# The sinks' part of a banded attention: from fp32 products a head to stacked fp32r products a pair of heads, with eight sinks beside a key block

## The chip, the cores and the metric

The kernel runs on one core of a Trainium2 chip. The metric is the device time of one execution in microseconds. The engines are TensorE (PE in the profile; its weight loads are PEld), VectorE (DVE), ScalarE (ACT), GpSimd (POOL) and SyncE (SP), which here only starts transfers. They run their own instruction queues in order and wait for each other by semaphores.

## What is computed

An attention with a few sink positions and a window, then two mixing blocks on its output. Two batches, 8 heads, 768 positions, 64 channels a head; `n_sink` is 4 and `window` 128.

```python
def _attn_ref(q, k, v, n_sink, window):
    scores = np.matmul(q, k.transpose(0, 1, 3, 2)) / np.sqrt(D)
    is_sink = pos[None, :] < int(n_sink)
    in_window = (rel >= 0) & (rel < int(window))      # rel = row - column
    scores = np.where(is_sink | in_window, scores, -1e9)
    a = np.exp(scores - np.max(scores, axis=-1, keepdims=True))
    a = a / (np.sum(a, axis=-1, keepdims=True) + 1e-09)
    return np.matmul(a, v)

def _moe_ref(x, w_in, w_spatial, b_spatial, w_out):   # on the heads side by side
    h = np.maximum(x @ w_in, 0.0)
    u, v = h[..., :512], h[..., 512:]
    v_n = (v - mean(v)) / np.sqrt(var(v) + 1e-06)
    return (u * (einsum('ts,bsd->btd', w_spatial, v_n) + b_spatial[:, None])) @ w_out

def _moe2_ref(x, w_tok1, w_tok2, w_ch1, w_ch2):
    h = np.maximum(x.transpose(0, 2, 1) @ w_tok1, 0.0) @ w_tok2
    u = x + h.transpose(0, 2, 1)
    return u + np.maximum(u @ w_ch1, 0.0) @ w_ch2
```

## The kernel before

*Attention.* `banded` works on 12 blocks j of 128 queries, 6 a batch (i = j mod 6). A block goes in two halves of four heads, so there are 24 groups g = 2j + ph. One loop over n from -3 to 25 is a software pipeline with a lag for each step: iteration n computes the scores of group n+3 (`qk`, L177, on TensorE; `scores`, L202 and L207, on DVE, which also gives the row minimum), the exponentials of group n+2 (`expo`, L223, on ACT, with the row sums), the reciprocal sums and the normalisation of group n+1 (`sums`, L184; `norm`, L234 on POOL for two heads, L238 on ACT for the other two), the transposes of group n and their copies out of PSUM (`a_transpose`, L253; `a_out`, L261 on ACT and L264 on DVE), and the products with the values of group n-1 (`pv`, L287). Each engine's queue has the order in which these lines are written (the schedule is by hand).

*Sinks.* A block with a predecessor (i > 0, ten of the twelve) needs the first positions of the sequence as well. The keys come from the host with `SK` = 16 sink keys behind each 128-key block, so a group of scores reads a run of 272 columns (288 where the ring of key blocks wraps). `norm` multiplies the sinks' weights by the reciprocal sums on POOL into a tile `eS` of 8 heads x 16 sinks = 128 columns (L242). In the odd iteration of a block `sinks` transposes `eS` (L296) into a PSUM tile that it shares by name ("fl", two slots) with the dense work, and ACT copies it to `aS` (L298). In the even iteration that follows, `sinks_mm` adds, for each of 8 heads, the product of `vs` (the sinks' values, with zeros where row and column belong to different heads, 128 rows deep, 64 columns of the head) with the whole of `aS` into the PSUM tile of the block (L306): fp32, two records each. `x_out` then writes the block's output as an fp32r high part (L315, ACT) and a low part (L316, DVE).

*Precision.* fp32r products round their operands, so the dense parts split each operand into a rounded high part and the remainder and add three products, high x high, high x low and low x high (`mm3`, L57 to L59). The attention's products are plain fp32.

*Around it.* Each iteration from -1 to 6 also prepares one weight slice (`pump`): three DVE operations on 512 columns (L464, L468, L471), and for the slice before it an ACT copy (L482) and a POOL subtract (L483) behind them. Dense work on finished blocks (`fill`, tiles psv and psu, L57 to L59) is put on TensorE's queue at the end of each iteration up to a fixed cost, so its place in the order doesn't depend on time. `step` runs pieces of a layer norm. Loads go by SP's queue, `load_v` with the sinks' values behind block 1 of each batch. What follows the loop is the dense part, `mlp`.

## Time and profile before

| | |
|---|---|
| time, median of 3 runs | 499.09 us (498.95 to 500.24) |
| profiled execution, its own time | 499.52 us |
| span of it, first to last instruction | 497.7 us |
| mean granted TensorE clock | 0.978 |
| TensorE, DVE, ACT, POOL busy | 95%, 56%, 35%, 29% of the span |

The profile is of one execution. A row of the groups by line gives the line, engine, operation, result and operands by the program's names, shapes, count, then the busy time in us, the mean of one in ns, and the idle time of the engine ahead of it. Matmuls overlap: a matmul's duration holds its way through the array, so its price in a stream is the spacing, which the chain of waits shows. A table by stretch gives from and to in us, the length, then busy time and count for PE, PEld, DVE, ACT and POOL in that order. A stretch's clock is the mean granted TensorE clock as a share of 2.4 GHz. A POOL or DVE duration may hold a wait for the other.

### The profile page before, as it was taken

How to read it: one execution, taken by the hardware profiler on the slowest of the kernel's cores; microseconds unless marked ns; L12 is line 12 of the kernel's file. 1: busy time of each engine (PE TensorE's matmuls, PEld its weight loads, DVE VectorE, ACT ScalarE, POOL GpSimd, SP SyncE). 2: the span in 40 equal slices, each digit the busy share in tenths (PEclk: the TensorE clock that was granted, in tenths of full speed). 3: DMA queues.
4: the chain of work that ended last, by engine and by line, in shares of the span. 5: the costliest groups of instructions: out<-in, count | busy, mean ns of one | idle time of the engine just before them, and what ended most of it. 6: DMA issues, size and time to landing. Idle time of an engine off the chain costs nothing.

```text
span 497.7 us, 7141 instructions
## 1 busy us (share of the span) xinstructions
PE 473.5 (95%) x2672; PEld 395.4 (79%) x2672; DVE 280.5 (56%) x631; ACT 176.5 (35%) x471; POOL 145.3 (29%) x164
## 2 busy tenths in 40 slices
PE   8589799999999999999999899999999999999994
PEld 7357588788888999998888578888888888888883
DVE  6989864675553489946979798765222211311112
ACT  4556677686754322235542222222101110011000
POOL 1453742354344557652543133222100000000000
PEclk9859899999999999999999999999999999999998
DMA  8844131402005022313544244221020000200002
GB/s 265 264 149 139 65 97 38 153 23 86 2 2 211 1 84 65 96 32 105 170 127 131 83 126 128 84 86 42 2 84 0 1 0 1 85 1 0 0 1 91
DMA packets 19788, 38.82 MB, mean 78 GB/s; under 512 B 1825, under 2 KB 8225, under 8 KB 19745
## 3 DMA queue, kind: packets, MB, share of 16 engines
q1 hardware_dynamic: 19312, 38.02, 24.1%
q8 instruction: 23, 0.38, 0.3%
q10 hardware_dynamic: 432, 0.26, 0.2%
q14 instruction: 21, 0.16, 0.1%
HBM read 35.13 MB, written 3.15 MB: 77 GB/s over the span
## 4 chain that ended last, share of the span: by engine, by line
PE 82%; DVE 13%; ACT 1%; issue 1%; DMA 1%; POOL 0%; POOLq 0%; ACTq 0%
PE pso L59 7%; PE pso L57 7%; PE pso L58 7%; PE psc L57 6%; PE psc L59 6%; PE psc L58 6%; PE pv L287 4%; PE psg L59 3%; PE psg L58 3%; PE psg L57 3%; PE sc L177 3%; DVE wi L468 2%; PE psu L57 2%; PE ps L59 2%; PE ps L57 2%; PE ps L58 2%
## 5 line engine op out<-in xcount | busy, mean ns | idle before, releaser
L630 DVE SCALAR_TENSOR_TENSOR hh<-psc,hh 128x512 fp32r<-128x512 f32 x36 | 24.9, 692 | 127.9 <-ACT hh L629 127.8
L629 ACT ACTIVATE hh<-psc 128x512 fp32r<-128x512 f32 x36 | 21.5, 597 | 157.1 <-PE psc L59 157.1
L59 PE MATMUL pso<-c2H,hh 128*128 128x512 f32 x144 | 56.3, 391 | 1.2 <-DVE hh L630 1.2
L57 PE MATMUL pso<-c2H,hh 128*128 128x512 f32 x144 | 56.8, 394 | 0.0
L58 PE MATMUL pso<-c2L,hh 128*128 128x512 f32 x144 | 56.1, 390 | 0.0
L471 DVE SCALAR_TENSOR_TENSOR wi<-rawi,wi 128x512 int32<-128x512 int32 (+2 forms) x46 | 41.2, 895 | 1.6
L223 ACT ACTIVATE e<-s,nm 128x144 f32<-128x144 f32 (+1 forms) x96 | 38.1, 399 | 4.0 <-DVE nm L207 4.0
L468 DVE SCALAR_TENSOR_TENSOR wi<-rawi,wi 128x512 int32<-128x512 int32 (+2 forms) x46 | 36.4, 791 | 1.6
L464 DVE TENSOR_SCALAR wi<-rawi 128x512 int32<-128x512 int32 (+2 forms) x46 | 32.8, 712 | 0.7 <-POOL c1L L483 0.6
L59 PEld LDWEIGHTS pso<-c2H,hh 128*128 128x128 f32 x144 | 27.0, 188 | 7.3 <-DVE hh L630 1.6
L57 PE MATMUL psg<-wsTH,vnH 128*128 128x384 f32 x96 | 32.1, 334 | 0.0
L58 PE MATMUL psg<-wsTL,vnH 128*128 128x384 f32 x96 | 32.1, 334 | 0.0
L59 PE MATMUL psg<-wsTH,vnL 128*128 128x384 f32 x96 | 32.1, 334 | 0.0
L58 PEld LDWEIGHTS pso<-c2L,hh 128*128 128x128 f32 x144 | 27.1, 188 | 5.4
L57 PEld LDWEIGHTS pso<-c2H,hh 128*128 128x128 f32 x144 | 27.1, 188 | 5.4
L177 PE MATMUL sc<-kr,q 64*128 64x272 f32 (+2 forms) x192 | 29.5, 424 | 1.1 <-DVE nm L207 0.7
L59 PE MATMUL psc<-u2H,c 128*128 128x512 f32 x72 | 28.0, 389 | 0.0
L57 PE MATMUL psc<-u2H,c1H 128*128 128x512 f32 x72 | 28.0, 389 | 0.0
L58 PE MATMUL psc<-u2L,c1H 128*128 128x512 f32 x72 | 28.0, 389 | 0.0
L59 PE MATMUL psc<-u2H,c1L 128*128 128x512 f32 x72 | 28.0, 389 | 0.0
L57 PE MATMUL psc<-u2H,c 128*128 128x512 f32 x72 | 28.0, 389 | 0.0
L58 PE MATMUL psc<-u2L,c 128*128 128x512 f32 x72 | 28.0, 389 | 0.0
(139 smaller groups left out, 1108.7 us busy)
## 6 DMA issues: line engine op xcount, KB each, us to landing
rawi<-in_moe_w_ch SPq DMA_DIRECT2D x24, 512.0 KB, 3.6
rawi<-in_moe_w_in SPq DMA_DIRECT2D x8, 512.0 KB, 4.7
kr<-in_k SPq DMA_DIRECT2D x11, 288.0 KB, 4.2
v<-in_v SPq DMA_DIRECT2D x12, 256.0 KB, 3.8
out_x<-o SPq DMA_DIRECT2D x12, 256.0 KB, 2.3
q<-in_q SPq DMA_DIRECT2D x11, 256.0 KB, 4.9
raws<-in_w_spT SPq DMA_DIRECT2D x6, 384.0 KB, 3.9
rawi<-in_moe_w_out SPq DMA_DIRECT2D x4, 512.0 KB, 5.0
```

Of the source, the lines that this page charges most:

```text
L57: self.nc.tensor.matmul(ps, lh, rh, start=(first and i == 0), stop=False)
L58: self.nc.tensor.matmul(ps, lh, rl, start=False, stop=False)
L59: self.nc.tensor.matmul(ps, ll, rh, start=False, stop=(last and i == n - 1))
L177: nc.tensor.matmul(o, q[r, p, :], k, start=True, stop=True)
L223: nc.scalar.activation(out=self.e[j][:, 4 * ph + c, :u], in_=s[:, c, :u], func=AF.Exp, bias=nm[:, c : c + 1], scale=-1.0, accum_out=sm[:, ...
L287: nc.tensor.matmul(ps[h * D : (h + 1) * D, p, :], w[:, (2 * p + h) * D : (2 * p + h + 1) * D], self.aT[g][c][:, 2 * x + h, :], start=(p == ...
L464: V.tensor_scalar(out=wi, in0=hi, scalar1=3, scalar2=0x3FFFFFFF, op0=ALU.logical_shift_left, op1=ALU.bitwise_and,)
L468: V.scalar_tensor_tensor(out=wi, in0=hi, scalar=-0x40000000, in1=wi, op0=ALU.bitwise_and, op1=ALU.bitwise_or)
L471: V.scalar_tensor_tensor(out=wi, in0=lo, scalar=29, in1=wi, op0=ALU.logical_shift_right, op1=ALU.bitwise_or)
L629: nc.scalar.activation(out=h, in_=ps, func=AF.Relu)
L630: nc.vector.scalar_tensor_tensor(out=l, in0=ps, scalar=0.0, in1=f32(h), op0=ALU.max, op1=ALU.subtract)
```

## The change

`SK` is 8. The sinks' values and weights are both split into a rounded part and a remainder, and the three products that `mm3` would add one after the other stand under each other along the contraction: 3 parts x 4 heads x 8 sinks = `SR` = 96 rows. The host gives `vs` with the same values in all three parts. `split_vs` (iterations 1 and 13) rounds it on ACT and writes the remainder into rows 32 to 63 on DVE; `load_v` puts the raw values into a slot of the pump's tiles. `norm` now normalises 136 columns in place where there are sinks, and `sink_parts` (even iterations of blocks with sinks, behind `v_step`) copies the sinks' weights out as rounded (ACT), rounded again (POOL) and remainder (POOL), in the order that meets the rows of `vs`. `sinks` makes two transposes, one for four heads, and one ACT copy of both; `sinks_mm` makes four fp32r products, one a pair of heads, 128 columns of `vs` with 128 of `aS`.

```diff
--- before.py
+++ after.py
@@ -22,7 +22,8 @@
 DTOK = 256
 DCH = 1536
 NF = DCH // P
-SK = 16
+SK = 8
+SR = 3 * 4 * SK
 KW = P + SK
 RING = 4
 NEG = 8.0e9
@@ -143,8 +144,18 @@
         self.vb[j] = self.ap.tile([P, DM], F32, name="v", tag="v", bufs=4)
         nc.sync.dma_start(out=self.vb[j], in_=self.v[b, i * P : (i + 1) * P])
         if i == 1:
-            self.vsb[b] = self.ap.tile([P, DM], F32, name="vs", tag="vs", bufs=1)
-            nc.sync.dma_start(out=self.vsb[b], in_=self.vs[b])
+            raw = self.sp.tile([P, DM], F32, name="vsraw", tag="tmp", bufs=4)
+            nc.sync.dma_start(out=raw[0:SR], in_=self.vs[b])
+            self.vsraw = raw
+
+    def split_vs(self, b):
+
+        nc = self.nc
+        raw = self.vsraw
+        t = self.vsb[b] = self.ap.tile([P, DM], F32R, name="vs", tag="vs", bufs=1)
+        nc.scalar.activation(out=t[0:SR], in_=raw[0:SR], func=AF.Copy)
+        r = slice(4 * SK, 8 * SK)
+        nc.vector.tensor_tensor(out=t[r], in0=raw[r], in1=f32(t[r]), op=ALU.subtract)
 
     def slots(self, j):
 
@@ -230,19 +241,22 @@
         nc = self.nc
         j, ph = divmod(g, 2)
         r = self.rs[g]
-        e = self.e[j][:, 4 * ph : 4 * ph + 4]
+        w = KW if j % NB else P
+        e = self.e[j][:, 4 * ph : 4 * ph + 4, 0:w]
         nc.gpsimd.tensor_tensor(
-            out=e[:, 2:4, 0:P], in0=e[:, 2:4, 0:P], in1=r[:, 2:4].unsqueeze(2).to_broadcast([P, 2, P]), op=ALU.mult
+            out=e[:, 2:4], in0=e[:, 2:4], in1=r[:, 2:4].unsqueeze(2).to_broadcast([P, 2, w]), op=ALU.mult
         )
         for c in range(2):
-            nc.scalar.activation(out=e[:, c, 0:P], in_=e[:, c, 0:P], func=AF.Copy, scale=r[:, c : c + 1])
-        if j % NB:
-            if ph == 0:
-                self.eS[j] = self.ap.tile([P, H, SK], F32, name="eS", tag="eS", bufs=2)
-            nc.gpsimd.tensor_tensor(
-                out=self.eS[j][:, 4 * ph : 4 * ph + 4], in0=e[:, :, P:KW],
-                in1=r.unsqueeze(2).to_broadcast([P, 4, SK]), op=ALU.mult,
-            )
+            nc.scalar.activation(out=e[:, c], in_=e[:, c], func=AF.Copy, scale=r[:, c : c + 1])
+
+    def sink_parts(self, j):
+
+        nc = self.nc
+        t = self.eS[j] = self.ap.tile([P, 2, 3, 4, SK], F32R, name="eS", tag="eS", bufs=1)
+        e = self.e[j].rearrange("p (g h) k -> p g h k", g=2)[:, :, :, P:KW]
+        nc.scalar.activation(out=t[:, :, 0], in_=e, func=AF.Copy)
+        nc.gpsimd.tensor_copy(t[:, :, 1], f32(t[:, :, 0]))
+        nc.gpsimd.tensor_tensor(out=t[:, :, 2], in0=e, in1=f32(t[:, :, 0]), op=ALU.subtract)
 
     def a_transpose(self, g):
         nc = self.nc
@@ -292,21 +306,21 @@
     def sinks(self, j):
 
         nc = self.nc
-        ps = self.pp.tile([P, 512], F32, name="fl", tag="fl")
-        nc.tensor.transpose(ps[:, 0:P], self.eS[j].rearrange("p h s -> p (h s)"), self.ident)
-        self.aS[j] = self.ap.tile([P, P], F32, name="aS", tag="aS", bufs=2)
-        nc.scalar.activation(out=self.aS[j], in_=ps[:, 0:P], func=AF.Copy)
+        ps = self.pp.tile([P, 2, P], F32, name="fl", tag="fl")
+        for g in range(2):
+            nc.tensor.transpose(ps[0:SR, g], f32(self.eS[j][:, g].rearrange("p t h s -> p (t h s)")), self.ident)
+        self.aS[j] = self.ap.tile([P, 2, P], F32R, name="aS", tag="aS", bufs=2)
+        nc.scalar.activation(out=self.aS[j][0:SR], in_=ps[0:SR], func=AF.Copy)
 
     def sinks_mm(self, j):
 
         nc = self.nc
         vs = self.vsb[j // NB]
         for p in range(NC4):
-            for h in range(2):
-                nc.tensor.matmul(
-                    self.ps_x[j][h * D : (h + 1) * D, p, :], vs[:, (2 * p + h) * D : (2 * p + h + 1) * D],
-                    self.aS[j], start=False, stop=True, skip_group_check=True,
-                )
+            nc.tensor.matmul(
+                self.ps_x[j][:, p, :], vs[0:SR, p * P : (p + 1) * P], self.aS[j][0:SR, p // 2],
+                start=False, stop=True, skip_group_check=True,
+            )
 
     def x_out(self, j):
         nc = self.nc
@@ -360,6 +374,9 @@
                 self.expo(n + LE)
             if 0 <= n < NG and ph == 0 and j % NB:
                 self.v_step(j)
+                self.sink_parts(j)
+            if n in (1, 13):
+                self.split_vs(n // 12)
             self.step()
             if n in PUMPS:
                 self.pump()
@@ -901,13 +918,15 @@
     )
     sinks = np.broadcast_to(k[:, 0:1, :, :, 0:SK], (B, NB, P, NC4, SK))
     v = np.asarray(inputs["v"]).transpose(0, 2, 1, 3)
-    vs = np.zeros((B, H, SK, H, D), v.dtype)
-    for h in range(H):
-        vs[:, h, :, h] = v[:, 0:SK, h]
+
+    vs = np.zeros((B, 3, 4, SK, 2, 4, D), v.dtype)
+    for h in range(4):
+        for g in range(2):
+            vs[:, :, h, :, g, h] = v[:, None, 0:SK, 4 * g + h]
     give("q", q)
     give("k", np.concatenate([k, sinks], axis=4))
     give("v", v.reshape(B, S, DM))
-    give("vs", vs.reshape(B, P, DM))
+    give("vs", vs.reshape(B, 3 * 4 * SK, DM))
     give("limits", np.array([inputs["n_sink"], inputs["window"]]).astype(np.int64))
     give("w_spT", np.asarray(inputs["moe_w_spatial"]).T)
     for name in _INS:
```

## Rows read from the trace of the kernel before

**Rows 1.** The page's first part: busy us (share of the span) x instructions.

```profile
PE 473.5 (95%) x2672; PEld 395.4 (79%) x2672; DVE 280.5 (56%) x631; ACT 176.5 (35%) x471; POOL 145.3 (29%) x164
```

**Rows 2.** By stretch: length, busy us and count by engine, granted clock, DMA.

```profile
20.00:30.00 10.00, 5.42 (x34) 2.94 (x35) 9.69 (x29) 6.30 (x23) 5.56 (x6) 0.78 0.61 190
30.00:36.00 6.00, 6.00 (x27) 4.74 (x28) 5.46 (x17) 2.97 (x12) 2.81 (x4) 0.51 0.28 87
...
61.00:145.00 84.00, 83.39 (x736) 68.02 (x734) 49.68 (x197) 57.29 (x195) 34.91 (x57) 1.00 0.18 59
```

**Rows 3.** Chain of waits by line: 7.5 to 57.5, then 61 to 145 us.

```profile
by line: DVE s L207 14.6%; DVE wi L468 13.7%; DVE wi L471 12.1%; DVE sc L202 9.9%; PE pv L287 7.1%; DVE r L184 5.3%; DVE wi L464 4.9%; DVE aL L264 4.8%; DVE xTL L316 3.7%; issue 3.5%; PE sc L177 3.2%; PE psv L58 2.6%; PE psv L57 2.6%; PE ps
...
by line: PE pv L287 18.5%; PE sc L177 15.5%; PE psu L57 8.9%; PE pv L306 8.3%; PE tr L253 8.2%; PE psv L57 8.0%; PE psu L59 6.9%; PE psv L59 6.9%; PE psu L58 6.9%; PE psv L58 6.8%; ACT e L223 1.9%; PE fl L296 1.9%; ACT e L238 0.8%; issue 0.
```

**Rows 4.** Chain of waits in order (start us, us, what), 56 to 91 us.

```profile
57.46 0.41 PE fl L296
...
63.44 0.87 PE pv L306 x16
...
64.97 0.23 PE psv L59
...
65.56 0.17 PE psu L59
...
70.01 0.17 ACT aS L298
...
82.60 0.44 PE tr L253 x4
83.04 1.12 PE sc L177 x8
...
89.29 1.17 PE sc L177 x8
```

**Rows 5.** By stretch again, L306 alone, 57.5 to 145 us (PE, PEld, clock, DMA).

```profile
57.50:145.00 87.50, 8.35 (x128) 7.26 (x128) 0.99 0.18 57
```

**Rows 6.** Groups by line (busy us, mean ns of one, idle before), whole execution.

```profile
L58 PEld LDWEIGHTS psu<-xTL,wuH 128*128 128x128 f32 x64 | 12.0, 188 | 0.1
...
L306 PEld LDWEIGHTS pv<-aS,vs 128*64 128x64 f32 x160 | 9.1, 137 | 0.0
...
L298 ACT ACTIVATE aS<-fl 128x128 f32<-128x128 f32 x10 | 2.6, 257 | 0.7 <-PE fl L296 0.7
```

**Rows 7.** DVE in order of time (start us, us, what), 8 to 62 us.

```profile
20.88 0.42 DVE L464 TENSOR_SCALAR wi<-rawi 128x512 int32<-128x512 int32 x1
...
22.07 0.69 DVE L471 SCALAR_TENSOR_TENSOR wi<-rawi,wi 128x512 int32<-128x512 int32 x1
22.68 1.23 DVE L184 TENSOR_SCALAR r<-sums 128x4 f32<-128x4 f32 x1
...
27.63 1.63 DVE L471 SCALAR_TENSOR_TENSOR wi<-rawi,wi 128x512 int32<-128x512 int32 x1
```

**Rows 8.** ACT in order of time, the same stretch.

```profile
21.43 0.62 ACT L482 ACTIVATE wvH<-wi 128x512 fp32r<-128x512 f32 x1
```

**Rows 9.** POOL in order of time, the same stretch.

```profile
22.13 1.76 POOL L483 TENSOR_TENSOR wvL<-wi,wvH 128x512 fp32r<-128x512 f32 x1 [2.04 <-ACT wvH L482]
...
24.77 0.29 POOL L242 TENSOR_TENSOR eS<-e,r 128x64 f32<-128x64 f32 x1
...
27.10 1.62 POOL L483 TENSOR_TENSOR wvL<-wi,wvH 128x512 fp32r<-128x512 f32 x1 [0.81 <-ACT wvH L482]
```

**Rows 10.** The tile of the sinks' values, vs: its transfers and their landing.

```profile
L147 SPq DMA_DIRECT2D vs<-in_vs x2: 327/328/328, 10.8 to 86.1; - x2
...
DMA to landing us min/median/max: 2.6/4.9/7.2
```

**Rows 11.** Groups by line and shape of DVE alone, 8 to 60 us.

```profile
L207 DVE CUSTOM_DVE_ANT_0 s<-sc,m 128x144 f32<-128x144 f32 x36 | 9.7, 305 | 0.6
...
L207 DVE CUSTOM_DVE_ANT_0 s<-sc,m 128x128 f32<-128x128 f32 x5 | 1.2, 286 | 0.2 <-PE sc L177 0.2
```


## The prediction

> **What bounds the kernel now.** I read the busy times first: TensorE is busy for 95% of the span and its weight loads for 79%, no other engine above 56% [rows 1]. That is an average, so next came the table by stretch [rows 2]. It shows two regimes in the only part that the change touches, the attention (up to 145 us). From about 8 to 57 us VectorE (DVE) is the full engine, 9.69 of 10 us in the third ten, while TensorE has holes. From 61 to 145 us TensorE is busy for 83.39 of 84 us and DVE for 49.68. The chain of waits says the same [rows 3]: ahead of 57.5 us its largest pieces are DVE's score and weight lines, behind 61 us it is nearly all TensorE. So there are two prices: in the first stretch a DVE microsecond counts and a TensorE one mostly doesn't, in the second it is the reverse. Behind 145 us the order of work is fixed and TensorE stays full, so what is won or lost before is handed on.
>
> An exception lies in the first stretch. From 30 to 36 us TensorE is the full one, at a granted clock of 0.51, that is at 1.2 of its 2.4 GHz [rows 2]. What starts that piece is a DVE result (the low part of x, L316), so it moves with DVE.
>
> **The change on TensorE.** *The products of the sinks* (L306). A block with a predecessor issues 8 fp32 products of 64 columns of weights, 16 records, and they take 0.87 us on the chain [rows 4]. Of ten such blocks eight lie behind 57.5 us (x128 at 16 a block, [rows 5]); the other two lie where DVE decides. The new form is 4 fp32r products, 96 rows deep, 128 columns of weights, 128 moving columns. The trace has no fp32r product that narrow. Lower end: 384 moving columns go by in 0.17 us and 512 in 0.23 [rows 4], so 128 columns are 0.06 us of streaming. Upper end: no better than fp32, where two halves together take 0.87/4 = 0.22 us. Between them stands the weight load. An fp32r load of 128 columns is 188 ns against 137 ns for 64 columns in fp32 [rows 6]; if the difference is the 64 columns more, a column is 0.8 ns and 128 of them 0.10 us, longer than the streaming, so each product waits for its load. A transpose, load and one pass of 128 columns, goes by in 0.44/4 = 0.11 us too [rows 4]. I take 0.11: 4 x 0.11 = 0.44 a block, a gain of 8 x 0.43 = 3.4 us. The ends are 8 x (0.87 - 0.24) = 5.0 and nothing.
>
> The Trainium skill has a rule that would give the lower end ("TensorE: Matmul & The Clock Gate", section on weight-path perf modes): a fast weight load is on when there are 128 weights and the type is not fp32. If fp32r counts as "not fp32", the load would fall behind the streaming. The trace speaks against it, since the 128-column fp32r load is the longer one, 188 ns [rows 6].
>
> *The transpose of the sinks* (L296) becomes two, of 96 columns each. One more is 0.11 us by the same transposes; the bound above is half of the 0.41 us that the lone one takes at half clock [rows 4], 0.21. Seven lie behind 61 us: +0.8 us (up to 1.5). Two more, at 31.9 and at 57.46 us, lie on the chain at half clock (0.41 us for the lone one, [rows 4]): +0.2 each, +0.4 us. The one at 44 us lies beside DVE's work: nothing.
>
> *The scores* (L177) read 264 key columns for 272. Groups with 288 columns take 1.17 us, with 272 they take 1.12 [rows 4]: 16 columns are 0.05, so 8 are 0.025 us. 11 groups behind 61 us: -0.3 us.
>
> *The copy of the transposed sinks* (ACT, L298) reads 256 elements for 128. The old one is 257 ns [rows 6], so the new one is 0 to 0.26 us longer. It ends a wait of TensorE for its PSUM slot, at 70.01 us on the chain [rows 4]; elsewhere the slot comes back in time. I take the middle once, +0.1 us; if the copy came last in each of the seven late blocks it would be up to 1.8.
>
> Sum behind 61 us: -3.4 + 0.8 - 0.3 + 0.1 = -2.8 us.
>
> **The change in DVE's stretch.** *The split of the weights* (split_vs) is issued in iteration 1 and again in 13, behind the exponentials and ahead of the weight pump. DVE's subtract needs ACT's rounded copy. In iteration 1 DVE is through with its scores at 20.9 us and goes straight on with the pump [rows 7]. ACT ends its exponentials at 21.43 and goes on with the pump's 512-element copy, 0.62 us [rows 8]; a copy of the same width now comes first, to 22.05. So DVE stands still for 1.15 us and then subtracts for 0.7 us (the price of its 512-element operations, as L471 at 22.07 us, [rows 7]): the pump's operations start at 22.75, not at 20.88. Behind the waiting DVE queue the three weight operations, the reciprocal sums of the next group, its scores, and with these ACT's and GpSimd's (POOL's) normalisation. What comes late next is POOL's subtract of the pump. It now starts at 22.65, not 22.13, and runs 1.3 us alone. Rows show that DVE's next operation on SBUF waits out such a subtract: L184 at 22.68 us takes 1.23 us and ends as POOL ends (22.13 + 1.76) [rows 7, 9], and so does L471 at 27.63. That stall is in the old time too; it now falls on L464, from 22.75 to 24.0, and the pump ends at 25.8, where the old order, stall included, was through with the sums at 23.9. Delay 2.0 us; at least the 1.15 + 0.7 less the part of the old stall that goes, say 1.3, at most 2.4. Nothing later takes it up: each wait from there to 57 us is behind a DVE result of that queue. The raw weights are no cause of a wait: their transfer, issued at 10.8 us, lands in 7.2 us [rows 10]. In iteration 13 the same work lies beside TensorE's, where DVE has some 34 us of slack [rows 2]: nothing. SP's queue no longer holds the second transfer, at 86.1 us [rows 10], until the old weights are read; that gains nothing either, since TensorE is full there.
>
> *The split of the sinks' weights* (sink_parts) adds in iterations 2, 4 and 6 (blocks 1 to 3) an ACT copy and two POOL operations; the POOL product of L242, 0.29 us [rows 9], goes for each group. The ACT copy waits for POOL's normalisation, which is done (24.2 + 0.6) long before ACT's exponentials. It puts the pump's copy, and with it POOL's subtract, back by some 0.25 us, and the two POOL operations of about 0.29 each fall on DVE's pump. Where the subtract holds DVE (27.10 to 28.72, L471 ending 29.26, [rows 7, 9]) a later subtract means a later DVE. From 0 (they fall into gaps) to 0.6 (DVE waits out both); I take 0.3 each, nearest to the 0.25 us by which the subtract moves: +0.9 us (0 to 1.8).
>
> The Trainium skill ("SBUF — State Buffer", section "Who interferes with whom") says that a DVE operation with two inputs in SBUF and a GpSimd operation that reads SBUF shut each other out for a whole instruction. By it alone, each of the six POOL operations would cost DVE its whole length and this term would be 1.8 us. The stall of L471 agrees [rows 7, 9]; that all six would come first at their meeting with DVE no row shows.
>
> *Narrower scores on DVE* (L207): 305 ns at 144 columns, 286 at 128, 36 of them [rows 11]: 10 ns each at 136, -0.35 us. The wider normalisation (136 columns for 128) costs ACT and POOL some 10 to 40 ns an instruction and lies behind DVE. The smaller transfers of keys and sinks gain nothing where no engine waits for them.
>
> Sum ahead of 61 us, with the cold transposes: 2.0 + 0.9 - 0.35 + 0.4 = +2.95 us.
>
> **Sum.** -2.8 + 2.95 = +0.15 us on the profiled execution's 499.52 us, 499.7. That execution lies 0.43 us above the median of the runs (499.09), so against the median: 499.2 us. By the bounds of its own terms (delay 1.3 to 2.4, POOL 0 to 1.8, late transposes 0.8 to 1.5) this case reaches from 499.2 - 0.7 - 0.9 = 497.6 to 499.2 + 0.4 + 0.9 + 0.7 = 501.2. Within 0.3%, about what a measurement of this kernel can tell from no change, is 497.6 to 500.6.
>
> **The rivals.**
> *A: a narrow fp32r product costs what fp32 costs* (slower). Then the change doesn't do what it says: 4 x 0.22 replaces 0.87, the gain of 3.4 is gone, and the second transposes and DVE's delay stay: 499.2 + 3.4 = 502.6 us. For it: no fp32r product below 384 columns is in the trace. Against: from 512 to 384 columns the price falls in proportion. It decides from 0.154 us a product ((0.154 - 0.11) x 32 = 1.4).
> *B: DVE's delay isn't handed on* (faster). In the half-clock piece at 30 to 36 us [rows 2] TensorE sets the end. If it runs there at full clock in the new order, some 2 to 3 us come back, which pays for the 2.0 + 0.9: 496.3 us. For it: the granted clock is 0.78, 0.51 and 1.00 in the three stretches of [rows 2], so it does change level around this piece, and the piece can fall otherwise. Against: the change gives TensorE more idle time ahead of it, not less.
> *C: streaming sets the price,* 0.06 a product: another 8 x 0.2 = 1.6 us, 497.6 us. It has the 188 ns of a weight load against it [rows 6]. The Trainium skill's fast weight load (above) would do this.
>
> **How the numbers follow.** Forecast 0.45, A 0.27, B 0.18, C 0.10. Faster by over 0.3%: most of B (0.17), half of C (0.05), a little of the forecast (0.04), 0.26. Slower: A (0.25) and the upper end of the forecast (0.07), 0.32. Within: 0.42. The range reaches to A's and B's times and leaves out some 0.2 beyond them: 496.4 to 502.8; the forecast's own is 497.6 to 501.2.
>
> **What would show it.** In the changed trace: the four fp32r products of a block spaced 0.11 us (0.06 is C, 0.22 A); a DVE subtract of the sink weights near 22 us behind a hole of about 1.1 us; the pump's subtracts on POOL some 0.3 us later in iterations 2, 4, 6; TensorE's full stretch starting about 3 us later than 57 us and, from there to the last x_out, shorter by 2.8. A stretch ahead of it that isn't longer, or a shorter run at half clock, makes the forecast wrong on the fast side; a wait of TensorE for the copies of the sinks in most late blocks, on the slow side.

## The result and the profile after

The changed kernel takes 495.19 us (median of 4 runs, 494.53 to 495.90) beside 499.29 us of the kernel before, measured with it (498.95 to 500.24): a ratio of 0.9909, 95% interval 0.9885 to 0.9934, so 3.3 to 5.7 us faster. The forecast was 499.2 us, and its range began at 496.4: the change is faster than the range allowed. The profiled execution of after took 494.53 us, 4.99 us less than that of before (499.52 us); its span is 492.7 us, the mean granted clock 0.984.

The first part of the page, against [rows 1]: busy us, share and instructions. TensorE has 110 products fewer and 4.6 us less busy time, and is still the full engine.

```profile
PE 468.9 (95%) x2562; PEld 391.6 (79%) x2562; DVE 279.7 (57%) x633; ACT 178.8 (36%) x483; POOL 146.7 (30%) x164
```

The table by stretch of after, with the columns of [rows 2] (busy us and count of PE, PEld, DVE, ACT, POOL, then the granted clock):

```profile
30.00:36.00 6.00, 5.46 (x33) 4.49 (x35) 5.83 (x17) 3.14 (x13) 3.31 (x3) 0.70 0.50 170
36.00:57.00 21.00, 18.18 (x140) 13.15 (x141) 20.35 (x65) 15.01 (x52) 14.61 (x18) 0.93 0.40 128
57.00:61.00 4.00, 4.00 (x34) 2.92 (x33) 2.82 (x15) 3.57 (x14) 2.77 (x3) 0.94 0.01 4
61.00:145.00 84.00, 83.20 (x650) 68.82 (x651) 51.69 (x200) 60.15 (x202) 36.72 (x58) 1.00 0.19 59
```

and two stretches of before that the prediction did not read:

```profile
36.00:57.00 21.00, 16.94 (x159) 12.52 (x159) 19.26 (x56) 13.10 (x44) 11.70 (x15) 0.98 0.40 129
57.00:61.00 4.00, 4.00 (x19) 3.00 (x16) 2.95 (x14) 2.96 (x12) 2.54 (x4) 0.66 0.02 6
```

Between 36 and 57 us DVE gets through 65 instructions where it got through 56: that stretch is ahead of the old order, not behind it. And the two pieces in which TensorE ran at or near half clock, 0.51 at 30 to 36 us [rows 2] and 0.66 at 57 to 61 us, now have 0.70 and 0.94.

To see where the time goes I compare one event in every run: the start of the transposes of iteration n on TensorE (tile tr, in TensorE's order of time). In before it lies at 24.84 us for n = 3, 35.89 for n = 4, 60.69 for n = 8 and 138.72 for n = 23. The table gives each profiled execution's difference to that, in us, and the kernel's median beside the median of before measured with it. All the kernels of the next section stand in it.

| kernel | n = 3 | n = 4 | n = 8 | n = 23 | median | before | ratio (95%) |
|---|---|---|---|---|---|---|---|
| after | +1.60 | -0.60 | -2.49 | -5.03 | 495.19 | 499.29 | 0.9909 (0.9885 to 0.9934) |
| e1_split | +2.18 | +2.26 | +2.27 | +2.23 | 501.46 | 499.36 | 1.0040 (1.0021 to 1.0058) |
| e2_parts | +0.07 | -1.28 | -2.19 | -2.21 | 496.52 | 499.36 | 0.9935 (0.9911 to 0.9958) |
| e3_before_warm | +0.03 | -2.64 | -3.14 | -3.16 | 497.55 | 499.36 | 0.9950 (0.9931 to 0.9968) |
| e4_after_warm | +1.90 | +1.75 | +0.03 | -2.32 | 494.73 | 499.36 | 0.9901 (0.9873 to 0.9930) |
| e5_sub_later | -1.03 | -0.20 | -2.71 | -3.74 | 495.80 | 500.25 | 0.9917 (0.9902 to 0.9932) |
| e5_parts_late | +2.22 | +0.90 | +1.92 | -0.60 | 498.61 | 500.25 | 0.9951 (0.9930 to 0.9971) |
| e6_flush_late | -0.02 | -2.59 | -1.42 | -1.41 | 499.37 | 500.25 | 0.9996 (0.9981 to 1.0010) |
| e7_pe_only | -0.78 | -3.28 | -3.95 | -6.68 | 494.86 | 500.25 | 0.9908 (0.9889 to 0.9928) |
| f1_before_next | -1.78 | -4.40 | -3.06 | -3.08 | 497.66 | 499.37 | 0.9957 (0.9939 to 0.9976) |
| f2_after_next | -0.39 | -1.16 | -4.72 | -7.19 | 493.37 | 499.37 | 0.9883 (0.9858 to 0.9908) |
| f3_after_next_warm | -0.32 | -3.07 | -5.77 | -8.29 | 490.99 | 499.37 | 0.9827 (0.9802 to 0.9852) |
| g1_sk8 | +0.03 | -1.19 | -1.28 | -0.72 | 499.57 | 499.73 | 0.9992 (0.9978 to 1.0006) |

In the row of after, half of the gain is made by iteration 8 (-2.49), where the forecast had +2.95, and half behind it (-5.03 + 2.49 = -2.54). The late half is as forecast: -2.8, or -2.4 up to this event, which the last block's products (0.43) follow. The early half has the wrong sign. These profiles are of single executions, which scatter around the median: that of e4 took 497.75 us, 3.0 more than its kernel's median, that of e2 498.14 us, 1.6 more. They scatter behind iteration 23 too, by up to 1.4 us: e3's span is 1.8 us shorter than that of before (495.9 for 497.7) though its iteration 23 starts 3.16 us earlier, f3's 9.0 us shorter with 8.29.

**The late half.** The chain of waits in order, after (start us, us, what), at places that answer to [rows 4]:

```profile
54.53 0.59 PE fl L311 x2
...
60.91 0.59 PE pv L320 x4
61.51 0.28 PE psv L58
...
67.06 0.28 ACT aS L313
...
117.38 0.35 PE fl L311 x2
```

and in before what stood behind the products, and the lone transpose at full clock:

```profile
64.31 0.43 PE psv L57
...
100.36 0.26 PE fl L296
```

The products and the first dense product behind them took 0.87 + 0.43 = 1.30 us and take 0.59 + 0.28 = 0.87 us: 0.43 us less a block. Both have to be read, since the dense product takes longer on the chain behind the old products than behind the new ones. The second transpose costs 0.35 - 0.26 = 0.09 us. One stretch of TensorE's weight loads and two groups by line of after, against [rows 6]:

```profile
101.53 0.52 PEld L320 LDWEIGHTS pv<-aS,vs 96*128 96x128 f32 x4 [0.17 <-issue]
...
L320 PEld LDWEIGHTS pv<-aS,vs 96*128 96x128 f32 x40 | 5.2, 190 | 1.7 <-issue 0.9 <-ACT e L234 0.7 <-ACT e L250 0.2
L313 ACT ACTIVATE aS<-fl 96x256 fp32r<-96x256 f32 x10 | 3.6, 363 | 0.8 <-PE fl L311 0.8
```

Four loads of 190 ns go by in 0.52 us: they are (0.52 - 0.19)/3 = 0.11 us apart. The copy of the transposed sinks takes 363 ns, 0.11 more than the old one.

**The early half.** DVE in order of time, after, with the hole and the subtract that the change adds, the pump behind it, and then the low part of x (xTL) in iterations 2, 4 and 6 with what stands around it:

```profile
21.84 0.68 DVE L158 TENSOR_TENSOR vs<-vsraw,vs 32x512 fp32r<-32x512 f32 x1 [1.13 <-ACT vs L156]
22.55 1.42 DVE L481 TENSOR_SCALAR wi<-rawi 128x512 int32<-128x512 int32 x1
...
29.20 0.69 DVE L488 SCALAR_TENSOR_TENSOR wi<-rawi,wi 128x512 int32<-128x512 int32 x1
29.81 0.68 DVE L330 TENSOR_TENSOR xTL<-pv,xTH 128x512 fp32r<-128x512 f32 x1
30.41 0.65 DVE L195 TENSOR_SCALAR r<-sums 128x4 f32<-128x4 f32 x1
...
40.20 0.69 DVE L488 SCALAR_TENSOR_TENSOR wi<-rawi,wi 128x512 int32<-128x512 int32 x1
40.81 0.68 DVE L330 TENSOR_TENSOR xTL<-pv,xTH 128x512 fp32r<-128x512 f32 x1
...
52.56 0.68 DVE L330 TENSOR_TENSOR xTL<-pv,xTH 128x512 fp32r<-128x512 f32 x1
```

The same places in before, beside [rows 7]:

```profile
29.19 0.68 DVE L316 TENSOR_TENSOR xTL<-pv,xTH 128x512 fp32r<-128x512 f32 x1
...
37.16 0.69 DVE L264 TENSOR_TENSOR aL<-tr,lowT 128x512 f32<-128x512 f32 x1 [1.53 <-ACT aT L261]
...
40.06 1.68 DVE L468 SCALAR_TENSOR_TENSOR wi<-rawi,wi 128x512 int32<-128x512 int32 x1
...
42.38 0.68 DVE L316 TENSOR_TENSOR xTL<-pv,xTH 128x512 fp32r<-128x512 f32 x1
...
53.57 1.64 DVE L471 SCALAR_TENSOR_TENSOR wi<-rawi,wi 128x512 int32<-128x512 int32 x1
55.13 0.68 DVE L316 TENSOR_TENSOR xTL<-pv,xTH 128x512 fp32r<-128x512 f32 x1
```

POOL in order of time, after, beside [rows 9], and then the POOL operation that stands ahead of xTL in iteration 6 of before:

```profile
28.49 0.84 POOL L259 TENSOR_TENSOR eS<-e,eS 128x64 fp32r<-128x64 f32 x1
29.31 1.73 POOL L500 TENSOR_TENSOR wvL<-wi,wvH 128x512 fp32r<-128x512 f32 x1
...
40.31 1.74 POOL L500 TENSOR_TENSOR wuL<-wi,wuH 128x512 fp32r<-128x512 f32 x1
...
53.04 1.61 POOL L534 TENSOR_TENSOR vnL<-vf,vnH 128x512 fp32r<-128x512 f32 x1 [0.81 <-ACT vnH L533]
```

In before, the pump's POOL subtract of iteration 2 starts at 27.10 us, ahead of DVE's last pump operation (27.63), which then takes 1.63 us instead of 0.69 [rows 7, 9], and xTL stands behind it. Iterations 4 and 6 have such a stall too, each in its own form. In 4 the middle one of the three pump operations waits (40.06), and the last one stands between it and xTL. In 6 the last one waits (53.57), and what holds it is not the pump's subtract but the layer norm's, L534 at 53.04. These are three stalls of 0.94 to 0.99 us, each in DVE's queue ahead of an xTL, for which TensorE's next products with the values wait. In after the new POOL subtract of the sinks' weights (L259, itself drawn out to 0.84 us beside DVE's L485) stands first in POOL's queue. The pump's subtract starts at 29.31, behind the start of DVE's L488 at 29.20. That one now takes 0.69 us, xTL follows at once, and what waits out POOL is the reciprocal sum behind it (30.41, 0.65 us, ending with POOL at 31.04; in iteration 6 again, 1.08 us at 53.97), or, at 40.31, nothing. So xTL, 2 us late at the start, is 0.62 us late in iteration 2 and 1.57 and 2.57 us early in iterations 4 and 6. The Trainium skill ("SBUF — State Buffer", section "Who interferes with whom") says that the order of issue, not the kind of operation, decides which of the two blocks; these rows agree (0.69 us for the same DVE operation where it starts 0.11 us ahead of POOL's, 1.63 where it starts 0.53 us behind).

A stall behind xTL costs less, since DVE's queue has to wait there in any case: in before 1.53 us at 37.16, for ACT's copy of the next transposes, which TensorE reaches only at the end of the products that xTL starts (and 1.91 us at 61.96, behind the xTL of iteration 6).

In these two executions the early half adds up. Iteration 3 starts 1.60 us late, the price of the split. With the first stall moved, xTL is 0.62 late. TensorE then takes 4.74 us from its first products behind xTL to the transposes of iteration 4, where before took 5.97: 1.23 less, and iteration 4 starts 0.60 early. With the other two stalls gone, xTL is 1.57 and 2.57 early, and iteration 8 starts 2.49 early. So some 2.9 us come from the stalls and 1.2 from that piece of TensorE's.

### The profile page after: what moved, and what is told of

Same layout as the page of the kernel before. It is cut to its first block, busy times and chain, and to the rows that moved or that the text cites. A ratio compares the mean times of both kernels' runs of the same rounds, so it can differ in the third digit from the quotient of the medians.

```text
span 492.7 us, 6952 instructions
## 1 busy us (share of the span) xinstructions
PE 468.9 (95%) x2562; PEld 391.6 (79%) x2562; DVE 279.7 (57%) x633; ACT 178.8 (36%) x483; POOL 146.7 (30%) x164
## 4 chain that ended last, share of the span: by engine, by line
PE 77%; DVE 14%; ACT 5%; issue 2%; POOL 1%; POOLq 0%; ACTq 0%
PE pso L60 7%; PE pso L58 7%; PE pso L59 7%; PE psc L60 6%; PE psc L58 6%; PE psc L59 6%; PE psg L58 3%; PE psg L60 3%; PE psg L59 3%; PE pv L301 3%; DVE wi L485 2%; PE ps L60 2%; PE ps L59 2%; PE ps L58 2%; ACT e L234 2%; PE psu L58 2%
## 5 line engine op out<-in xcount | busy, mean ns | idle before, releaser
L488 DVE SCALAR_TENSOR_TENSOR wi<-rawi,wi 128x512 int32<-128x512 int32 (+2 forms) x46 | 40.3, 876 | 1.6
L234 ACT ACTIVATE e<-s,nm 128x136 f32<-128x136 f32 (+1 forms) x96 | 37.6, 393 | 3.9 <-DVE nm L218 3.9
L485 DVE SCALAR_TENSOR_TENSOR wi<-rawi,wi 128x512 int32<-128x512 int32 (+2 forms) x46 | 36.4, 790 | 1.6
L481 DVE TENSOR_SCALAR wi<-rawi 128x512 int32<-128x512 int32 (+2 forms) x46 | 32.5, 707 | 1.4 <-POOL c1L L500 1.2
L188 PE MATMUL sc<-kr,q 64*128 64x264 f32 (+2 forms) x192 | 28.7, 417 | 0.4 <-DVE nm L218 0.2
```

Of the source, the lines that this page charges most:

```text
L188: nc.tensor.matmul(o, q[r, p, :], k, start=True, stop=True)
L234: nc.scalar.activation(out=self.e[j][:, 4 * ph + c, :u], in_=s[:, c, :u], func=AF.Exp, bias=nm[:, c : c + 1], scale=-1.0, accum_out=sm[:, ...
L481: V.tensor_scalar(out=wi, in0=hi, scalar1=3, scalar2=0x3FFFFFFF, op0=ALU.logical_shift_left, op1=ALU.bitwise_and,)
L485: V.scalar_tensor_tensor(out=wi, in0=hi, scalar=-0x40000000, in1=wi, op0=ALU.bitwise_and, op1=ALU.bitwise_or)
L488: V.scalar_tensor_tensor(out=wi, in0=lo, scalar=29, in1=wi, op0=ALU.logical_shift_right, op1=ALU.bitwise_or)
```

## The experiments

The first theory after the result was that the delay of `split_vs` is real and handed on, and that something in the early stretch gives back more: either the two POOL operations, by where they put the pump's subtract, or the clock in the piece from 30 to 36 us. The first four kernels take these one at a time. Of each edit the text shows the lines that matter; `...` stands for the rest, and what stands behind a # is a note of this text.

**e1_split**: before, with the work of `split_vs` alone. The raw values land in a slot of the pump's tiles, and iterations 1 and 13 issue

```diff
...
+nc.scalar.activation(out=t, in_=raw, func=AF.Copy)
+nc.vector.tensor_tensor(out=raw[32:64], in0=raw[32:64], in1=t[32:64], op=ALU.subtract)
```

> The kernel before with the weights' split alone: the sinks' values are loaded into a pump tile, ACT copies them (512 columns) and DVE subtracts 32 rows x 512 columns in iterations 1 and 13, at the places of the change; the products stay fp32. Theory 'handed on' (the prediction's step): DVE's delay of 2.0 us in iteration 1 reaches the end, 501.3 us against 499.3. Rival 'taken up': the delay moves GpSimd's pump subtracts and TensorE's clock so that most of it comes back by 60 us, within 1 us of the kernel before.

Measured: 501.46 us, +2.1. The delay is there from iteration 3 on and stays to the end within 0.1 us (+2.18, +2.26, +2.27, +2.23): nothing takes it up. The term of the forecast (+2.0) holds, size and handing-on both (1.0 to 2.9 us by the interval).

**e2_parts**: before, with the ACT copy and the two POOL operations of `sink_parts` at their places, their results unused:

```diff
...
+nc.scalar.activation(out=t[:, :, 0], in_=e, func=AF.Copy)
+nc.gpsimd.tensor_copy(t[:, :, 1], f32(t[:, :, 0]))
+nc.gpsimd.tensor_tensor(out=t[:, :, 1], in0=e, in1=f32(t[:, :, 0]), op=ALU.subtract)
```

> The kernel before with the sinks' weights split beside (one ACT copy and two GpSimd operations of 128x64 in the even iterations of blocks with sinks, behind v_step, results unused; GpSimd's old product for the sinks stays too). Prediction's step: +0.9 us, 500.2. Rival 'the subtract is moved past DVE's operations': the pump's subtract of iterations 2, 4 and 6 starts later and meets DVE operations that it doesn't hold, so about 1 us a stall goes in two or three of them: -1 to -2 us, 497.3 to 498.3.

Measured: 496.52 us, 2.8 us less for added work. DVE in order of time, of this kernel, in iterations 2 and 4, then POOL in iteration 2:

```profile
27.70 0.69 DVE L481 SCALAR_TENSOR_TENSOR wi<-rawi,wi 128x512 int32<-128x512 int32 x1
28.32 0.68 DVE L325 TENSOR_TENSOR xTL<-pv,xTH 128x512 fp32r<-128x512 f32 x1
...
39.58 1.66 DVE L481 SCALAR_TENSOR_TENSOR wi<-rawi,wi 128x512 int32<-128x512 int32 x1
...
27.12 0.73 POOL L156 TENSOR_TENSOR eD<-e,eD 128x64 fp32r<-128x64 f32 x1
27.80 1.73 POOL L493 TENSOR_TENSOR wvL<-wi,wvH 128x512 fp32r<-128x512 f32 x1
```

Iteration 2 has the pattern of after without its delay: POOL's subtract at 27.80 for 27.10 [rows 9], DVE's operation at 27.70 with 0.69 us for 1.63 [rows 7], xTL at 28.32 for 29.19. Iteration 6 has it as well, with xTL at 52.95 for 55.13. In iteration 4 this execution still has its stall, 1.66 us at 39.58, and xTL's 41.16 for 42.38 is only what was won before. So two of the three stalls moved here, some 1.9 us; TensorE's piece behind the first xTL gave 0.4 more (5.56 us for 5.97); together they are the -2.19 of iteration 8. The kernel's executions lie between 495.23 and 499.13 us; that the faster ones have lost the stall of iteration 4 too is likely but not shown. The edit also leaves the tile eS one buffer for two, for which POOL waits 0.97 us at 31.51; after has one buffer as well, and so has e5_parts_late below, which loses the gain. These POOL operations are the step of the forecast that failed: their term was +0.9.

**e3_before_warm** and **e4_after_warm**: unused products with the identity ahead of `pv` in the early iterations, to see what the clock is worth, in before and in after.

```diff
...
+WARM = {0: 6, 1: 8, 2: 8, 3: 10, 7: 10}
...
+            if n in WARM:
+                self.warm(WARM[n])
```

> The kernel before with unused fp32 products of the identity (6, 8, 8, 10 and 10 of 128x128) ahead of the value products in iterations 0, 1, 2, 3 and 7, where TensorE has holes. Theory 'clock': the half-clock pieces at 30 to 36 and 57 to 61 us run at full clock, 12 products at 0.2 us and some more, -2 to -3 us, 496.3 to 497.3. Theory 'the clock decides little': within 0.7 us of the kernel before, or slower by what the fillers take.

> The changed kernel with the same fillers. If the clock explains some 2 us of what the change gained, this one gains less from the fillers than the kernel before does (-1 us, 494.2) and the two filled kernels differ by about 2 us only. If the clock explains nothing, both gain or lose alike and they differ by the 4.1 us of the change.

Measured: 497.55 us, 1.8 us less than before by the medians (1.6 to 3.4 by the ratio's interval), and 494.73 us (0.9901), no more than after gains without the fillers (0.9909). The stretch from 30 to 36 us of e3, then the fillers of iteration 3 in e4, in TensorE's order of time:

```profile
30.00:36.00 6.00, 6.00 (x58) 4.79 (x60) 5.80 (x18) 3.81 (x14) 2.74 (x4) 1.00 0.30 90
...
29.72 4.62 PE L338 MATMUL warm<-ident 128*128 128x128 f32 x20
```

In e3 the fillers hold the clock at 1.00 here and at 57 to 61 us, so the 1.8 us are the worth of both half-clock pieces in before, less than what the forecast's rival B had for the first alone (2 to 3). Iteration 4 starts 2.64 us earlier, but its xTL only 1.62 (40.76 for 42.38). In e4's profiled execution the fillers themselves ran at half clock (0.51 from 29.72 to 34.27 us), took 4.62 us where e3's took 2.50, and held up the products behind xTL until 34.27 us. The two kernels with fillers differ by 2.8 us, the two without by 4.1. That lies between what was expected if the clock explains 2 us of the gain and if it explains nothing.

**e5_sub_later** and **e5_parts_late**: after, with one of the two early edits moved. In the first, DVE's subtract of the split comes an iteration later, so that it doesn't wait for ACT; in the second, the two POOL operations of `sink_parts` are issued behind the pump.

```diff
# e5_sub_later
...
-        nc.vector.tensor_tensor(out=t[r], in0=raw[r], in1=f32(t[r]), op=ALU.subtract)
...
+            if n in (2, 14):
+                self.split_low()                 # the same subtract
# e5_parts_late
...
+            if 0 <= n < NG and ph == 0 and j % NB:
+                self.sink_parts_pool()           # behind pump(), no longer ahead of it
```

> The changed kernel with DVE's subtract of the split issued one iteration later (2 and 14, ACT's copy stays in 1 and 13), so DVE doesn't stand still for ACT. If a delay of DVE in iteration 1 reaches the end, as the split alone showed (+2.1 us), the hole of 1.1 us is saved: 494.1 us. If the rest of the change takes it up: no difference from 495.2.

> The changed kernel with the two GpSimd operations of sink_parts issued behind the pump instead of ahead of it; ACT's copy stays where it was. Theory 'the pump's subtract is moved past the operations that TensorE waits for': it starts earlier again, DVE stands still ahead of the low part of x in iterations 2 and 6, and most of what the parts alone gained (2.8 us) is lost: 497 to 498 us. Rival 'the gain of the parts comes from elsewhere' (the single eS tile, ACT's copy, chance in the clock): within 0.7 us of 495.2.

Measured: 495.80 us (0.9917, after 0.9909) and 498.61 us (0.9951, that is 2.1 us slower than after; the two intervals just meet). DVE in order of time, of e5_sub_later and then of e5_parts_late:

```profile
27.44 1.65 DVE L494 SCALAR_TENSOR_TENSOR wi<-rawi,wi 128x512 int32<-128x512 int32 x1
29.01 0.68 DVE L334 TENSOR_TENSOR xTL<-pv,xTH 128x512 fp32r<-128x512 f32 x1
...
29.82 1.63 DVE L496 SCALAR_TENSOR_TENSOR wi<-rawi,wi 128x512 int32<-128x512 int32 x1
31.37 0.68 DVE L336 TENSOR_TENSOR xTL<-pv,xTH 128x512 fp32r<-128x512 f32 x1
```

The second is the clean one: same work, same engine, only POOL's order, and the stall is back ahead of xTL in iterations 2, 4 (41.65, 1.65 us) and 6 (54.33, 1.63 us), with xTL at 31.37, 43.22 and 55.89 us where after has 29.81, 40.81 and 52.56. Of the first difference (1.56 us) 0.62 was there in iteration 3's start, ahead of the edit; the other 0.94 is the stall. TensorE's piece behind that xTL ran as in after (4.69 us at a clock of 0.69, for 4.74 at 0.68), so the clock does not make the difference. The order on POOL is the cause. The first was expected to win and did not: the hole is gone (iteration 3 is 2.63 us earlier than in after), but with it the chance of the meeting changed, the stall is back at 27.44 and again at 40.57 (1.65 us), the subtract now takes its 0.72 us in iteration 2 (25.50), TensorE's piece behind xTL took 5.95 us at a clock of 0.53, and by iteration 4 it is 0.40 us later than after. By iteration 8 it is 0.22 us ahead again, and then it loses 1.5 us up to iteration 23, nearly all of it in two waits of TensorE. One is for ACT's copy of the transposed sinks, for whose PSUM slot the dense products wait; TensorE in order of time, of this kernel:

```profile
68.03 0.44 PE L58 MATMUL psu<-xTH,wuH 128*128 128x384 f32 x1 [1.28 <-ACT aS L317]
```

After waits 0.57 us there. The other is for xTL at 107.28 us, 0.75 us for 0.16. An earlier start does not spare TensorE what ACT and DVE deliver late.

**e6_flush_late**: before, with the pump's ACT copy and POOL subtract issued behind `x_out`, to move the stall without adding work.

```diff
...
-            self.flush()
+            if hold:
+                self.held = self.half            # flushed behind x_out
...
```

> The kernel before with the pump's ACT copy and GpSimd subtract issued behind x_out instead of ahead of it, nothing added. Theory as above: the subtract can't stand between DVE and the low part of x, so the gain of the parts comes without them, 496 to 497.5 us against 499.3. Rival: within 0.7 us of the kernel before.

Measured: 499.37 us, no change. The edit did not do what it was made for, as DVE of this kernel shows:

```profile
27.61 1.75 DVE L476 SCALAR_TENSOR_TENSOR wi<-rawi,wi 128x512 int32<-128x512 int32 x1
```

The stall is still ahead of xTL (29.29), so it says nothing on that. It shows one other thing: its clock at 30 to 36 us was 1.00, for which nothing in the edit was meant, and iteration 4 started 2.59 us earlier, but its xTL only 1.46 (40.92 for 42.38). That is about the 1.53 us for which DVE had waited in before, and DVE has no more to give. By iteration 8 it is 1.42, and the time shows nothing of it. A gain by the clock in that piece is partly given back while DVE is the full engine.

**e7_pe_only**: after without the remainders: no subtract on DVE, no operation on POOL; the other two parts of the weights are zero.

```diff
...
-        nc.vector.tensor_tensor(out=t[r], in0=raw[r], in1=f32(t[r]), op=ALU.subtract)
...
-        t = self.eS[j] = self.ap.tile([P, 2, 3, 4, SK], F32R, name="eS", tag="eS", bufs=1)
-        nc.gpsimd.tensor_copy(t[:, :, 1], f32(t[:, :, 0]))
-        nc.gpsimd.tensor_tensor(out=t[:, :, 2], in0=e, in1=f32(t[:, :, 0]), op=ALU.subtract)
+        t = self.eS[j] = self.eS0                # set to zero once
```

> The changed kernel without the remainders: DVE's subtract of the weights and the two GpSimd operations of sink_parts are left out, the second and third part of the sinks' weights are zero, so the low-order terms are missing from the output; TensorE's work is that of the change. By the terms of the sum (late -2.8, narrower scores -0.35, cold transposes +0.4) it is 2.75 us faster than the kernel before: 496.6. By the two parts as measured alone (split +2.1, parts -2.8 of the change's -4.1) it is 3.4 us faster: 495.9, a little less for ACT's copies that stay.

Measured: 494.86 us (0.9908). From iteration 8 to 23 it gains 6.68 - 3.95 = 2.73 us: the late half again, and with the other kernels that have the new products (after 2.54, e4 2.35, e5_parts_late 2.52, f2 2.47, f3 2.52) the best-settled number of the study; only e5_sub_later, with its two waits, has less (1.03). Its early part gains 3.95 us, and not by the stalls, which all three stand ahead of xTL again (1.63 us at 26.96, 1.64 at 38.37 and 51.07). It ran at full clock there, 1.00 at 30 to 36 and at 57 to 61 us.

**f1_before_next, f2_after_next, f3_after_next_warm**: if the place of the stall is the cause, it can be moved on purpose. In before (f1) and in after (f2), the pump's POOL subtract of iterations 0 to 2 and 4 to 6 is issued one iteration later, behind the normalisation; f3 is f2 with the fillers of e4.

```diff
...
+            self.flush_low()                     # the POOL subtract held back, behind norm(n + LN)
...
-                self.pump()
+                self.pump(hold=n in (0, 1, 2, 4, 5, 6))
```

> The kernel before with the pump's GpSimd subtract (only that, in iterations 0 to 2 and 4 to 6) issued one iteration later, behind the normalisation of the next group, where DVE reads its scores out of PSUM; nothing added, ACT's copy stays. Theory 'what pays is where GpSimd's subtract meets DVE': the stalls of about 1 us on DVE go in six of seven iterations, the low part of x comes 2 us and more earlier, -2 to -4 us, 495.5 to 497.5. Rival 'it is the clock alone': no more than 1 us from the kernel before.

> The changed kernel with the same edit. By the theory most of the stalls that it had left (iterations 0, 3 and 5, and the one of 1.42 us on the first pump operation of iteration 1) go too: -1.5 to -3 us, 492.5 to 494; in the even iterations the value difference of GpSimd still meets the pump. If the change had already taken what there was to take: within 0.7 us of 495.2.

> The changed kernel with the same edit and the unused products that keep TensorE's clock up. If clock and stalls add, this is the fastest of all, 491.5 to 493; if DVE alone sets the end ahead of 60 us once the stalls are gone, it equals the one without the fillers.

Measured: 497.66, 493.37 and 490.99 us. DVE of f1, in order of time:

```profile
24.66 1.44 DVE L465 TENSOR_SCALAR wi<-rawi 128x512 int32<-128x512 int32 x1
...
27.47 0.68 DVE L316 TENSOR_TENSOR xTL<-pv,xTH 128x512 fp32r<-128x512 f32 x1
...
47.27 1.44 DVE L465 TENSOR_SCALAR wi<-rawi 128x512 int32<-128x512 int32 x1
48.74 1.64 DVE L469 SCALAR_TENSOR_TENSOR wi<-rawi,wi 128x512 int32<-128x512 int32 x1
```

With none of the change's work, before gains 2.1 us by its ratio: of DVE's six stalls beside POOL between 20 and 57 us four are left, and xTL of iteration 2 starts at 27.47 us for 29.19. The pump's last operation is free ahead of every xTL. But three of the four still lie in DVE's queue ahead of one, further forward (24.66 in iteration 2, 47.27 and 48.74 in iteration 6): at 24.66 and 47.27 POOL's product of the values (dv) meets the pump. So this run shows that fewer stalls pay, and not by itself that their place does. On after, the same edit gains another 1.3 us by the ratios (0.9909 to 0.9883), which their intervals do not tell from nothing. With the fillers as well the clock holds, 1.00 from 20 to 145 us, as f3 by stretch shows for one piece,

```profile
30.00:36.00 6.00, 6.00 (x54) 4.64 (x50) 5.83 (x18) 4.25 (x16) 4.16 (x5) 1.00 0.26 85
```

and that is worth 493.37 - 490.99 = 2.4 us. f3 is the fastest of all, 1.7% below before.

**g1_sk8**: before with eight sinks for 16 and nothing else; its fp32 products are 64 rows deep for 128.

```diff
-SK = 16
+SK = 8
+HS = 8 * SK
...
-                    self.aS[j], start=False, stop=True, skip_group_check=True,
+                    self.aS[j][0:HS], start=False, stop=True, skip_group_check=True,
```

> The kernel before with eight sinks beside a key block and nothing else: the fp32 products are 64 rows deep, 16 records a block as before, one transpose. By the prediction's rows: narrower scores on DVE -0.35 us, narrower key runs on TensorE -0.3 us, 498.7 against 499.3. If a product's price followed its depth, some 4 us more would go (495).

Measured: 499.57 us beside 499.73 (0.9992, interval 0.9978 to 1.0006). The narrower scores are worth less than the comparison can tell; the 0.35 + 0.3 us of the forecast lie within its interval. Halving the depth of the products is not worth anything that shows. In its profile iteration 4 starts 1.19 us earlier than in before with xTL at the same time, 29.19 us; that is the clock again (next section).

## Why the prediction was right and where it failed

**The products on TensorE: right.** The spacing is 0.11 us, the value taken; 0.06 (rival C) and 0.22 (rival A) are both refuted. A block saves 0.43 us, as forecast, with some luck: the four products take 0.59 us on the chain, not 0.44, and the 0.15 come back in the dense product behind them (0.28 for 0.43), which the sum left out. The argument from the weight load fits (at 190 ns a load is as long as those of [rows 6], and no faster); no run tests it apart from the spacing. The rule of the Trainium skill that would have given C ("TensorE: Matmul & The Clock Gate", section on weight-path perf modes) does not show here: if fp32r counts as "not fp32", 190 ns for 128 columns in fp32r against 137 for 64 in fp32 [rows 6] is no fast load, and the products stand 0.11 us apart, not at the 0.06 of streaming.

**The second transposes and the copy: right, in small.** 0.09 us against 0.11; the cold pair at 54.53 us in after takes 0.59 us for 0.41 [rows 4], +0.18 against +0.2. The copy is 0.11 us longer and stands on the chain of waits twice, at 67.06 and 77.25 us (once in before, [rows 4]); +0.1 was the term, taken once. The sum behind iteration 8 is -2.54 us where -2.4 was forecast for the same stretch.

**The split of the values: right.** The hole is 1.13 us (forecast 1.15), the subtract 0.68 (0.7), and the stall falls on L481 (1.42 us at 22.55), as written. Its price, alone, is +2.1 us and it is handed on to the end (e1_split).

**The POOL operations of the sinks: wrong in sign.** The term was +0.9 us and measured -2.8 (e2_parts; 2.1 to 4.4 less by the interval). The step that failed is the sentence "a later subtract means a later DVE". It priced the stall as if the subtract, moved back, would hold the same DVE operation until later. But a meeting of the two has an order: whichever starts first runs through. Moved back by 0.7 us in e2_parts and 2.2 in after (27.10 to 27.80 and 29.31), the subtract came behind the start of DVE's last pump operation, and the stall of 0.94 to 0.99 us went to the reciprocal sum behind xTL or nowhere, in all three iterations of after and in two of e2_parts. The row that could have told this was in view: DVE's L471 at 27.63 began only 0.53 us behind POOL's 27.10 [rows 7, 9], so the forecast's own shift of 0.25 us, together with the two POOL operations that it named "of about 0.29 each" and put ahead of the subtract, carried it past that start. The lower bound of the term should have been three stalls given back, -2.9 us, not 0. The rule on who shuts out whom, cited in the prediction, was used for the price (1.8 us) and not for the order.

**"Nothing later takes it up": true of the delay, wrong of the sum.** e1's delay is never taken up. In after it is, because the moved stalls give back more than the delay. The reason given, that each wait up to 57 us is behind a DVE result, passes over the wait of 1.53 us at 37.16, which is for ACT and TensorE: what comes late ahead of xTL is handed on, what comes late behind it need not be.

**Rival B** gave 496.3 us, the nearest, and the range, which was meant to reach to B's time, began 0.1 us above it. Its condition, the clock in the piece at 30 to 36 us, was half met (0.70 for 0.51). TensorE in order of time, before, then after, and behind these the stretch from the first products behind xTL of iteration 2 to the transposes of iteration 4 in before, after, e6_flush_late and g1_sk8:

```profile
29.92 0.69 PE L287 MATMUL pv<-aT,v 128*64 128x128 f32 x4 [1.97 <-DVE xTL L316]
...
30.55 0.69 PE L301 MATMUL pv<-aT,v 128*64 128x128 f32 x4 [1.05 <-DVE xTL L330]
...
29.92:35.89 5.97, 5.97 (x26) 4.71 (x27) 5.50 (x18) 2.97 (x12) 2.70 (x4) 0.51 0.28 88
...
30.55:35.29 4.74, 4.74 (x27) 3.95 (x28) 4.57 (x16) 3.07 (x12) 2.17 (x3) 0.68 0.51 170
...
30.02:33.30 3.28, 3.28 (x26) 2.67 (x27) 3.14 (x15) 2.95 (x12) 0.92 (x3) 1.00 0.49 160
...
29.93:34.70 4.77, 4.77 (x27) 3.71 (x27) 4.60 (x16) 2.94 (x12) 2.40 (x3) 0.64 0.38 110
```

TensorE is busy all through, with the same products but for one or two, and the time goes by the granted clock: 5.97 us at 0.51, 4.77 at 0.64, 4.74 at 0.68, 3.28 at 1.00. So the 1.2 us that after gains in this piece, in this execution, are the clock's. Whether the change raises that clock is not shown: e6 and g1 had 1.00 and 0.64 there with no edit that was meant for it. On the whole time it can have done little. The 71 executions of before under 502 us that stand beside the experiments took 498.2 to 498.7 us at a mean granted clock of 0.988 and 500.4 to 500.9 at 0.975; those at 0.981 to 0.984, where after's four lie, have a median of 499.05 us, 3.9 above that of after. And e2_parts is no faster by its clock: 0.980 on the mean, as before has.

**Do the parts add up?** By medians: the split +2.1, the POOL operations -2.8, eight sinks -0.2, the late half -2.5: -3.4 us, where the change measures -4.1 (3.3 to 5.7 by its interval). The 0.7 left are within the uncertainty of the parts, and so is what is counted twice, since the late half has a share of the narrower scores in it. e7 does not fit as well: its -4.6 us by the ratio with the split's +2.1 and the POOL operations' -2.8 put back would be -5.3. e7 keeps the ACT copies and has neither of the others, so its early 3.95 us have no counted cause but the full clock. That difference of 1.2 us stays open.

## What to carry to other kernels

An added operation on an engine that can shut out the bottleneck engine, as POOL and DVE do each other here, is to be priced by what it does to the order of the next meeting, and not only by its length: list each pair that excludes each other with its two starting times, and where the gap is smaller than the shift, put both signs into the bounds. Then look at what stands directly behind the stalled instruction: the same 0.95 us cost the time of the kernel ahead of xTL, for which TensorE waits, and little behind it, where DVE has a wait of its own (1.53 us at 37.16 in before). And a stall that is found in such a list can be moved by issuing the off-path operation an iteration later, which brought 2.1 us to the old kernel (f1) and, with the clock held by fillers, made the fastest one here.

## What the chip showed that was not expected

- A DVE operation with a single small operand, the reciprocal sum on 128x4 elements, waits out a POOL subtract as well: 0.65 us at 30.41 in after and 1.08 at 53.97, 0.14 to 0.17 in most places without one. xTL, with one input in PSUM, does not: 0.68 us beside POOL's subtract at 40.81 as without it. POOL is held in its turn: its subtract of 128x64 elements took 0.84 us at 28.49 beside DVE's L485, and 0.32 at 62.00 without.
- The price of an fp32 product did not follow the depth of its contraction: 64 rows for 128 in all ten blocks gave 499.57 us for 499.73 (g1_sk8).
- Work that does nothing made the kernel faster three times: the unused POOL operations by 2.8 us (e2_parts) and the unused products by some 2 us (e3_before_warm) and 2.4 us (f3 against f2), where the granted clock at 30 to 36 us went from 0.51 and 0.69 to 1.00.
- The granted clock of one and the same stretch of products was 0.51, 0.64 and 1.00 in three kernels whose work ahead of it is nearly the same (before, g1_sk8, e6_flush_late), and it took 5.97, 4.77 and 3.28 us. A difference of one or two microseconds between two single profiles of this kernel can be that alone.
